# The short block's two output tiles: one tile's additions made first, and its rows sent in transfers of 64 on two queues

## The chip, the cores and the metric

One core of one Trainium2 chip runs the whole program. The metric is the device time of one execution in microseconds (us), taken as the median of several runs. The engines are PE (matrix products), DVE (vector), ACT (scalar), POOL (GpSimd) and SP (the sync engine, which here issues every DMA).

## The reference

Attention with a positional bias over 4 batches, 8 heads, 576 positions and head size 64, then two feed-forward layers over the 4 x 576 = 2304 tokens. Only the last one matters here:

```python
def _moe2_ref(x, w_in, w_out):           # x: (2304, 512), w_in: (512, 2048), w_out: (2048, 512)
    h = x @ w_in
    g = where(h >= 1, h, where(h <= -1, 0, (h + 1) ** 2 / 4))
    return g @ w_out                      # float32, (2304, 512)
```

## The kernel before, in words

The 576 positions are cut into five blocks (`BLK`, line 126): four of 128 positions, and the short one of 64 (`SJ`, number 4). The last layer takes the blocks in the order 0, 1, 2, 3, 4 (`ORDER`, line 808), the short one last. A block has its 128 positions of all four batches, so 512 tokens; the short one has 64 of each batch, so 256 tokens.

Block 0 is done by `h2_mm`, `g_mid`, `out_mm` and `out_store`. The others are done by halves (a "unit" below: 256 tokens; two units for each of blocks 1 to 3 and one for block 4, seven in all) with a seven-product scheme in the manner of Strassen. For each unit the loop at line 1146 runs over eight pairs of the hidden columns (`q`):

- `g_pair` (lines 1091 to 1113): PE makes the hidden values (`h2_half`, line 1085, 24 matmuls of 128x256 for a pair, into the three PSUM tiles `pm`); ACT and DVE apply the function (1102 to 1104); POOL makes four sums (1106 to 1109); ACT and DVE split the seven operands into two fp16 parts (1111, 1112).
- `out7` (line 1124): 21 matmuls of 128x256 add into the seven products m0 to m6. It runs two pairs behind `g_pair` (`gl=2`). The products lie in four PSUM banks, two tiles called `s`: m0 to m3 in one, m4 to m6 in the other. There are only these two tiles, so the next unit's first matmul into either must wait until the unit before has been read out of it.
- `store7` (lines 1126 to 1139), after the last pair of a unit: ACT copies m0, scaled, to SBUF (1133). DVE then makes seven additions (1136), each of 128x256, that form the two output tiles o1 and o2 of 128 rows x 512 columns. o2's right half, after the first addition, is a sum that others read, and it is overwritten by a later one. Then SP issues one transfer for each tile (1139).

In blocks 1 to 3 an output tile has 128 positions of one batch (`nr` = 128, `reps` = 1). In block 4 it holds 64 positions of two batches (`nr` = 64, `reps` = 2), so that transfer's pattern is 2 x 64 rows of 2 KB: the outer step goes from one batch to the next.

The instructions of each engine run in the order that a planner writes at build time; it goes by program order as priority and by its own forecast of when each instruction is ready. So DVE's additions for a unit can have other work between them.

Of the kernel before, what the change touches and what calls it, by code (L numbers as in the profile page):

```python
# [20 lines left out]
def kernel(ctx: ExitStack, tc: tile.TileContext, qt, kt, vr, small, mw1, mw2, mw3, mwo, win, wo2, out):  # L21
# [7 lines left out]
    V, A, G, T, SP = nc.vector, nc.scalar, nc.gpsimd, nc.tensor, nc.sync  # L29
    P = 128  # L30
    B, H, S, D = 4, 8, 576, 64
# [62 lines left out]
    def st(shape, dt, tag):  # L94
        return sb.tile(shape, dt, tag=tag, name=tag, bufs=BUFS.get(tag, 1))
# [69 lines left out]
    if True:  # L165
# [73 lines left out]
        for j in range(5):  # L239
            i0, n = BLK[j][0], BLK[j][1]  # L240
# [885 lines left out]
        def store7(y, sub, m, g):  # L1126
            i0, nr, n = BLK[ORDER[y]]
            k = c_ko[:, g:g + 1]
            o1, o2 = part[2 * (gcount[1] % 2)], part[2 * (gcount[1] % 2) + 1]
            gcount[1] += 1  # L1130
            lo, hi = slice(0, 256), slice(256, 512)
            m1 = st([P, S], F32, "sp")[:, :256]
            A.activation(m1, m[0], AF.Copy, scale=k)
            for dst, x, add in ((o2[:, hi], 1, m1), (o1[:, lo], 2, m1), (o2[:, lo], 3, o2[:, hi]), (o1[:, hi], 4, o2[:, hi]),
                                (o2[:, hi], 4, o2[:, lo]), (o1[:, hi], 5, o1[:, hi]), (o2[:, lo], 6, o2[:, lo])):
                V.scalar_tensor_tensor(dst, m[x], k, add, ALU.mult, ALU.add)
            reps = P // nr
            for c, o in ((2 * sub, o1), (2 * sub + 1, o2)):
                SP.dma_start(out.rearrange("(b i) d -> b i d", b=B)[c * reps:c * reps + reps, i0:i0 + nr], o)

        gcount.append(0)
        work = [(0, 0, ft) for ft in range(NF2)] + [(y, sub, q) for y in range(1, 5) for sub in range(BLK[ORDER[y]][2] // 256) for q in range(NP)]
# [3 lines left out]
        for x in range(len(work) + GL):  # L1146
# [19 lines left out]
            if x >= GL:  # L1166
                y, sub, ft = work[x - GL]
                if y == 0:
                    if ft % GROUP == 0:
                        accs[0] = acc4()  # L1170
                    end = ft % GROUP == GROUP - 1
                    out_mm(ORDER[0], ft, gls.pop(x - GL), accs[0], ft % GROUP == 0, end)
                    if end:
                        out_store(0, accs.pop(0), ft // GROUP, ft == GROUP - 1, ft == NF2 - 1)
                else:
                    if ft == 0:
                        accs[y] = [a[:, 256 * i:256 * i + 256] for a in acc4() for i in range(2)]
                    out7(ft, gls.pop(x - GL), accs[y], ft == 0, ft == NP - 1)
                    if ft == NP - 1:
                        store7(y, sub, accs.pop(y), NP - 1 + y)  # L1180
# [35 lines left out]
```

## Time and profile before

| | us |
|---|---|
| median of 3 runs | 1039.41 |
| lowest and highest of them | 1038.9, 1041.57 |
| the profiled execution | 1050.42 |
| its span, first to last instruction | 1048.6 |
| busy in the span: PE | 945.8 |
| DVE | 720.8 |
| ACT | 600.3 |
| POOL | 496.4 |

The profiled execution is 11.0 us longer than the median of the runs. Its span is 1.8 us shorter than its own time. Every time with a position in it ("at 1034.44") is counted from the first instruction of the span.

### The profile page before, as it was taken

How to read it: one execution, taken by the hardware profiler on the slowest of the kernel's cores; microseconds unless marked ns; L12 is line 12 of the kernel's file. 1: busy time of each engine (PE TensorE's matmuls, PEld its weight loads, DVE VectorE, ACT ScalarE, POOL GpSimd, SP SyncE). 2: the span in 40 equal slices, each digit the busy share in tenths (PEclk: the TensorE clock that was granted, in tenths of full speed). 3: DMA queues.
4: the chain of work that ended last, by engine and by line, in shares of the span. 5: the costliest groups of instructions: out<-in, count | busy, mean ns of one | idle time of the engine just before them, and what ended most of it. 6: DMA issues, size and time to landing. Idle time of an engine off the chain costs nothing. (4 is left out here: it accounts for less than half of the span.)

```text
span 1048.6 us, 25979 instructions
## 1 busy us (share of the span) xinstructions
PE 945.8 (90%) x10258; PEld 767.8 (73%) x10258; DVE 720.8 (69%) x1614; ACT 600.3 (57%) x1194; POOL 496.4 (47%) x721
## 2 busy tenths in 40 slices
PE   5779788798999999989899888989999999999993
PEld 5547667677888878777677777534588888888882
DVE  8977777776556677546455587898786677676662
ACT  4688864864565645768577687443344344344441
POOL 1022487665667764646457101976034344344340
PEclk7667889989999999999989999999999999999997
DMA  9795998998799978999989753010020010000000
GB/s 299 219 269 119 251 205 213 190 214 209 154 226 213 196 180 188 208 219 232 211 160 195 195 205 105 21 41 1 1 81 22 2 41 22 2 21 21 2 22 20
DMA packets 238910, 141.47 MB, mean 135 GB/s; under 512 B 187460, under 2 KB 217668, under 8 KB 238276
## 3 DMA queue, kind: packets, MB, share of 16 engines
q1 hardware_dynamic: 238788, 139.81, 57.3%
q8 instruction: 80, 1.31, 0.5%
q14 instruction: 42, 0.34, 0.1%
HBM read 79.68 MB, written 15.27 MB: 91 GB/s over the span
## 5 line engine op out<-in xcount | busy, mean ns | idle before, releaser
L775 PEld LDWEIGHTS <-aw 128*128 128x128 f16 x2160 | 193.2, 101 | 49.7 <-issue 28.2
L775 PE MATMUL pm<-xT,aw 128*128 128x256 f16 (+1 forms) x1944 | 219.6, 267 | 10.6 <-ACT hl L802 3.0
L698 POOL TENSOR_TENSOR phl<-sp,phl 128x512 f16<-128x512 f32 x136 | 161.5, 1188 | 0.0
L680 ACT ACTIVATE sp<-sp,mx 128x576 f32<-128x576 f32 x144 | 110.6, 768 | 79.9 <-DVE mx L678 79.5
L697 POOL TENSOR_TENSOR phl<-sp,phl 128x64 f16<-128x64 f32 x136 | 47.1, 346 | 208.8 <-ACT phl L696 132.8
L664 PE MATMUL s<-k,qz 64*128 64x288 f32 (+1 forms) x576 | 135.0, 458 | 10.3 <-DVE mx L678 8.2
L1102 ACT ACTIVATE sp<-pm,vec 128x256 f32<-128x256 f32 x112 | 61.3, 556 | 93.1 <-PE pm L1085 93.0
L678 DVE CUSTOM_DVE_ANT_0 sp<-s,ab 128x576 f32<-128x576 f32 x128 | 93.5, 752 | 30.5 <-POOL phl L698 12.6
L720 PEld LDWEIGHTS <-pt 128*128 128x128 f16 x1792 | 75.4, 102 | 35.2 <-DMA pt<-phl 22.7
L664 PEld LDWEIGHTS s<-k,qz 64*128 64x128 f32 (+1 forms) x576 | 72.7, 199 | 32.6 <-DVE mx L678 12.1
L696 ACT ACTIVATE phl<-sp 128x576 f16<-128x576 f32 x136 | 89.9, 673 | 3.3 <-DMA pt<-phl 2.5
L720 PE MATMUL pav<-v,pt 128*128 128x64 f16 x1568 | 72.8, 198 | 15.6 <-DMA pt<-phl 15.3
L797 PE MATMUL pm<-hh,wo 128*128 128x256 f16 x648 | 77.1, 273 | 6.7 <-ACT hl L802 3.1
L1085 PEld LDWEIGHTS <-ab 128*128 128x128 f16 x756 | 73.8, 98 | 9.4
L1106 POOL TENSOR_TENSOR hh<-hh 128x128 f32<-128x128 f32 x56 | 30.2, 540 | 106.3 <-DVE hh L1104 101.4
L1103 DVE SCALAR_TENSOR_TENSOR hh<-pm,vec,sp 128x256 f32<-128x256 f32 x112 | 52.7, 479 | 34.2 <-ACT sp L1102 34.0
L797 PEld LDWEIGHTS <-wo 128*128 128x128 f16 x648 | 61.6, 98 | 16.9 <-issue 9.3
L787 POOL TENSOR_TENSOR hh<-hm,hh 128x256 f16<-128x256 f32 (+1 forms) x60 | 43.0, 716 | 62.3 <-ACT hh L786 60.9
L782 DVE SCALAR_TENSOR_TENSOR hm<-pm,hm 128x256 f32<-128x256 f32 (+1 forms) x120 | 47.1, 393 | 33.9 <-PE pm L775 14.0
L1124 PEld LDWEIGHTS <-xT 128*128 128x128 f16 x588 | 57.5, 98 | 7.8 <-ACT xT L1111 1.2
L1124 PEld LDWEIGHTS <-wo 128*128 128x128 f16 x588 | 57.5, 98 | 6.7
L1107 POOL TENSOR_TENSOR hh<-hh 128x128 f32<-128x128 f32 x56 | 25.8, 460 | 72.6 <-DVE hh L1104 67.9
(281 smaller groups left out, 1990.4 us busy)
## 6 DMA issues: line engine op xcount, KB each, us to landing
k<-in_k_dram SPq DMA_DIRECT2D x64, 288.0 KB, 4.1
v<-v_d SPq DMA_DIRECT2D x24, 640.0 KB, 5.0
ws<-in_moe_w_out_dram SPq DMA_DIRECT2D x15, 512.0 KB, 5.0
ws<-in_moe_w_in_dram SPq DMA_DIRECT2D x9, 512.0 KB, 4.5
x_d<-hl SPq DMA_DIRECT2D x36, 128.0 KB, 3.0
qz<-in_q_dram SPq DMA_DIRECT2D x16, 256.0 KB, 5.3
ab<-in_moe_w_dram SPq DMA_DIRECT2D x8, 512.0 KB, 8.8
qz<-x_d SPq DMA_DIRECT2D x4, 1024.0 KB, 4.8
```

Of the source, the lines that this page charges most:

```text
L664: last_score[0] = T.matmul(sbox[i + r][:, c, :288], q[p, s if u.j == SJ else s // 2], k[p, 288 * c:288 * c + 288], start=True, stop=True)
L678: V.tensor_tensor_reduce(halves(sn), sbox.pop(i)[:, :, :288], halves(bias_sb[u.j][:, h]), -0.125, 3e38, ALU.add, ALU.min, mx)
L680: last_soft[0] = A.activation(pf, sn, AF.Exp, scale=-1.0, bias=mx, accum_out=u.sums[:, h:h + 1])
L696: A.activation(hl[:, :S], pf, AF.Copy)
L698: G.tensor_tensor(hl[:, S + 64:], pf[:, :512], hl[:, :512], ALU.subtract)
L720: T.matmul(u.pav[:, 64 * h:64 * h + 64], pt[:, c], v[:, sl, 64 * (h % 4):64 * (h % 4) + 64], **kw)
L775: T.matmul(o, wm[:, ft, i, wp, kk], x_rhs(key, xp, kk) if n == 256 else x_rhs(key, xp, kk)[:, c], start=(x == 0), stop=(x == 11))
L797: T.matmul(pm, wo16[:, ft, wp, P * d:P * d + P], hh[:, ft, hp], start=(ft == 0 and y == 0), stop=(ft == NF1 - 1 and y == 2))
L1085: T.matmul(pm, w[:, wp, kk], x2t[ORDER[y]][:, kk, xp, 256 * sub:256 * sub + 256], start=(x == 0), stop=(x == 11))
L1102: A.activation(r, pm, AF.Relu, scale=c_ch[:, f], bias=c_half)
L1103: V.scalar_tensor_tensor(t, pm, c_c[:, f], r, ALU.mult, ALU.max)
L1124: T.matmul(m[x], gl[:, gp, i], w[:, wp], start=(start and z == 0 and x % 2 == 0), stop=(stop and z == 2 and (x % 2 == 1 or x == 6)))
```

## The change

In `store7` the seven additions are put into another order, in all seven units: the ones that complete o1 come as numbers 2, 3 and 4, and the other three of o2 follow. The operands of each are the same. Each output tile is sent by one transfer for each batch in it: the first from SP, the second, if there is one, from ACT. Where `reps` is 1 (blocks 1 to 3) that is again one transfer of 128 rows from SP. In block 4 it is two transfers of 64 rows x 2 KB for each tile, one from SP and one from ACT, four instead of two.

```diff
-            for dst, x, add in ((o2[:, hi], 1, m1), (o1[:, lo], 2, m1), (o2[:, lo], 3, o2[:, hi]), (o1[:, hi], 4, o2[:, hi]),
-                                (o2[:, hi], 4, o2[:, lo]), (o1[:, hi], 5, o1[:, hi]), (o2[:, lo], 6, o2[:, lo])):
+            for dst, x, add in ((o2[:, hi], 1, m1), (o1[:, lo], 2, m1), (o1[:, hi], 4, o2[:, hi]), (o1[:, hi], 5, o1[:, hi]),
+                                (o2[:, lo], 3, o2[:, hi]), (o2[:, hi], 4, o2[:, lo]), (o2[:, lo], 6, o2[:, lo])):
                 V.scalar_tensor_tensor(dst, m[x], k, add, ALU.mult, ALU.add)
             reps = P // nr
             for c, o in ((2 * sub, o1), (2 * sub + 1, o2)):
-                SP.dma_start(out.rearrange("(b i) d -> b i d", b=B)[c * reps:c * reps + reps, i0:i0 + nr], o)
+                for r in range(reps):
+                    (A if r else SP).dma_start(out.rearrange("(b i) d -> b i d", b=B)[c * reps + r, i0:i0 + nr], o[nr * r:nr * r + nr])
```

Here `A` is ACT, `V` is DVE, `SP` the sync engine, `lo` and `hi` the left and right 256 columns; the second item of each entry is the number of the product.

## Rows read from the trace of the kernel before

**Rows 1.** Busy time by stage: us, PE, PEld, DVE, ACT, POOL, PEclk, DMA share, GB/s.

```profile
1000.00:1030.00 30.00, 29.12 (x268) 25.87 (x266) 17.95 (x31) 11.36 (x17) 12.47 (x24) 1.00 0.05 19
1030.00:1048.60 18.60, 1.56 (x15) 1.16 (x12) 3.15 (x8) 0.47 (x1) 0.00 (x0) 0.64 0.08 28
```

**Rows 2.** The chain that ended last, its end: start, us, what.

```profile
1031.33 0.48 ACT sp L1133
...
1031.84 1.67 DVE hm L1136 x4
...
1033.54 0.88 DVE hm L1136 x2
```

**Rows 3.** Timeline from 1034 on: start, us, engine, line, what.

```profile
1033.54 1.27 DVE L1136 SCALAR_TENSOR_TENSOR hm<-s,vec,hm 128x256 f32<-128x256 f32 x3
1034.44 1.30 SPq L1139 DMA_DIRECT2D out_dram<-hm  x2
```

**Rows 4.** What SP waited for after 1030: line, releaser, us, times, longest.

```profile
SPq L1212 <- DMA out_dram<-hm: 11.8, 1, 11.8
```

**Rows 5.** The DMA view from 1034 to 1049, 40 slices of 0.375 us.

```profile
DMA  0000010110111111111111111111111111100000
GB/s 0 0 0 0 22 22 22 33 33 22 22 44 44 55 49 49 55 49 49 55 49 49 55 49 49 55 55 44 55 55 49 49 55 49 49 11 0 0 0 0
DMA packets 260, 0.52 MB, mean 35 GB/s; under 512 B 4, under 2 KB 4, under 8 KB 260
```

**Rows 6.** The DMA view of a 128-row unit, 842.3 to 848, slices of 0.1425 us.

```profile
DMA  0000002799960000000499993000000000000000
GB/s 0 0 0 0 0 0 86 302 402 417 388 230 15 0 0 0 0 0 0 187 388 417 388 359 101 0 0 0 0 0 0 0 0 0 0 0 0 0 0 0
DMA packets 288, 0.52 MB, mean 92 GB/s; under 512 B 32, under 2 KB 32, under 8 KB 288
out_dram<-hh SPq DMA_DIRECT2D x2, 256.0 KB, 2.0
```

**Rows 7.** Line 1139: ns of an issue (min/median/max), first and last start; landing.

```profile
L1139 SPq DMA_DIRECT2D out_dram<-hm x8: 332/332/667, 803.1 to 1035.2; - x8
DMA to landing us min/median/max: 2.0/2.0/4.0
```

**Rows 8.** Line 310, 64-row loads at the program's start: ns of an issue; landing.

```profile
L310 SPq DMA_DIRECT2D ws<-in_v_dram x6: 487/1199/5053, 6.3 to 113.7; - x6
DMA to landing us min/median/max: 7.6/9.4/12.7
```

**Rows 9.** The program's first transfer and its first reader, in the timeline.

```profile
0.74 0.40 SPq L168 DMA_DIRECT2D sm<-in_small_dram  x1
2.57 0.23 DVE L205 TENSOR_SCALAR sc<-sm 128x8 f32<-128x8 f32 x1 [1.63 <-DMA sm<-in_small_dram]
```

**Rows 10.** Timeline of the first changeover between units, without POOL.

```profile
801.02 0.87 DVE L1136 SCALAR_TENSOR_TENSOR hm<-s,vec,hm 128x256 f32<-128x256 f32 x2
...
802.25 0.87 DVE L1136 SCALAR_TENSOR_TENSOR hm<-s,vec,hm 128x256 f32<-128x256 f32 x2
...
803.39 0.49 PE L1124 MATMUL s<-ab,wo 128*128 128x256 f16 x3
...
804.42 0.48 DVE L1136 SCALAR_TENSOR_TENSOR hm<-s,vec,hm 128x256 f32<-128x256 f32 x1
...
806.23 0.49 PE L1124 MATMUL s<-ab,wo 128*128 128x256 f16 x3
```

**Rows 11.** Line 1124: PE's waits (ns, first and last start) and its idle time.

```profile
L1124 PEldq EVENT_SEMAPHORE x6: 51/51/51, 801.5 to 998.3; - x6
its engine sat idle before it (us, times) until:
  ACT xT L1111: 2.0, 2
```

## The prediction

> **What bounds the kernel now.** I began with the busy time by stage, because a single bound for the whole span would mislead here. Up to 1030 PE is the bound: between 1000 and 1030 it is busy 29.12 of 30 us. In the last 18.6 us it works 1.56 us, DVE 3.15, ACT 0.47, and POOL nothing [rows 1]. So the program ends with some 14 us in which no engine computes, and whatever shortens that stretch shortens the program us for us.
>
> Next the end of the chain of waits and the timeline. ACT copies m0 at 1031.33; DVE's seven additions run from 1031.84 without other work among them [rows 2] and end at 1033.54 + 1.27 = 1034.81. SP issues the first tile's transfer at 1034.44 and is through with the second at 1034.44 + 1.30 = 1035.74 [rows 3]. From there SP waits 11.8 us, in one piece, for the output to land [rows 4], to about 1047.6; the closing steps take the remaining 1.0 us to 1048.6. That wait is the target.
>
> Is 11.8 us what 512 KB costs? The DMA view says no. In this stretch the DMA share is a steady 1 tenth, at about 52 GB/s, and 512 KB at 52 GB/s is 10.1 us [rows 5]. A unit of 128 positions sends the same 512 KB in two transfers of 256 KB at shares of 9 tenths and up to 417 GB/s, each within about 1 us, and each lands 2.0 us after its issue [rows 6]. 417 over 52 is 8, and two of sixteen engines is an eighth. The small packets say the same: 32 for two transfers there, which I read as one completion from each of 16 engines; 4 for two transfers here, two engines each [rows 5, 6]. The transfers differ in one thing: 128 rows against 2 x 64 rows. So the short block's data go through two DMA engines because the outer step of their pattern has two values, and both tiles queue on the same two.
>
> **The change part by part.** *The transfers.* Two transfers of 2 x 64 rows go; four of 64 rows come. I take a 64-row pattern to spread over the sixteen engines as a 128-row one does. Then o2's two halves are together the size of one 128-row transfer, 256 KB, and at 417 GB/s that is 0.6 us of traffic [rows 6]; issue to landing I take as 2.0 us, the median of the 128-row transfers of this line, whose extreme is 4.0 [rows 7]. One half alone has fewer bytes, but both share the engines. The only 64-row transfers in the trace are loads at the program's start, issue to landing 7.6 to 12.7 us [rows 8]; they stood behind megabytes of other loads, while at the end nothing else moves. So the bounds are 2.0 and 12.7, and I take the near one, since the nearest row in place, size and direction is that of the same output.
>
> The Trainium skill speaks against this part (DMA: Bandwidth & Descriptors, section "Rules for kernel authors"): of two transfers to disjoint partition halves it says "Don't bother — they serialize", one transfer of 128 partitions being better. Taken as it stands, that rule leaves the end at 1039.4; it supposes halves and whole on the same sixteen engines, and the trace shows the whole on two. The same page (section "Why a DMA increments its semaphore by 16 and not by 1") lets the outermost step choose the engines: 2 gives two, and 64 would give sixteen. The 2 and the 128 agree with the completions counted above; no row shows a 64-row transfer in the clear.
>
> *The second queue.* ACT has issued no transfer before. Its issue cost is not in the trace; SP's lie between 0.33 and 0.67 us for this line [rows 7], and being shorter could not bring the end forward by more than 0.33. I take SP's 0.33. A first use of a queue is bounded by SP's own: issued at 0.74, used at 2.57, so 1.83 us in all [rows 9], no more than a warm one. ACT has nothing after the copy of m0 [rows 2], so nothing is queued behind its waits; SP has nothing behind these transfers but the final wait.
>
> *The order of the additions.* An addition that waits for nothing new begins 0.40 us after the one before: three in 1.27 us with 0.48 for the last, (1.27 - 0.48) / 2 [rows 3, 10]. The fourth began at 1031.84 + 3 x 0.40 = 1033.04, the fifth at 1033.54 [rows 2]: 0.50, because it overwrites what the fourth reads. So an addition that depends on its direct predecessor costs 0.10 more. Before there is one such; after there are three (o1's right half twice, o2's left half into its right half, and that read before the left half is overwritten). The last addition ends at 1034.81 + 0.20 = 1035.01. o1 is complete after the fourth instead of the sixth addition, at about 1033.6 instead of 1034.4; but o2 comes last, so this brings nothing to the end beyond keeping both queues free. If the planner puts another addition between, the 0.20 is not paid.
>
> *The sum.* o2's transfers are issued at 1035.04 (0.03 after the last addition, as now) and land at 1037.04, against 1047.6. That is 10.5 us less; the closing steps stay at 1.0. Profiled execution: 1050.42 - 10.5 = 1039.9. It stands 11.0 us above the median of the runs; its extra time I take to lie outside this stretch, since the rate of two engines doesn't depend on being watched: 1039.41 - 10.5 = 1028.9.
>
> *The six other units.* Their transfers keep pattern and queue. The new order also works where PE is the bound. The next unit's products need the PSUM tiles. In the first changeover the third addition, the last reader of m0 to m3, begins at 801.02 and ends 0.48 later, at 801.5, which is where PE's wait stands [rows 10, 11], and PE uses that tile at 803.39: 1.9 us of slack. After the change m3 is read by the fifth addition. That now starts at 802.25, ending at 802.7, still 0.7 us early; the cover is PE's work on the next pairs' hidden values. The last addition ends at 804.90 and its tile is used at 806.23, a slack of 1.3 us against a delay of at most 0.2 [rows 10]. PE's idle time before line 1124 is 2.0 us in all, and none of it is put down to the additions [rows 11]. I take nothing for these units.
>
> **The rivals.**
>
> *Changeovers cost a little.* The planner already leaves the last addition until 804.42, 1.3 us after the sixth ended [rows 10]. If it does that to o2's three additions, m3 is read at about 804.9 at the latest, 1.5 us after PE wants the tile. If PE's other work fills half of that, six changeovers cost 6 x 0.75 = 4.5 us: 1033.4. For it: three additions in place of one can be pushed behind other work. Against: their program order is still ahead of the next unit's.
>
> *Slower.* The same mechanism in full, at its place, the release of m0 to m3. Each changeover would have to cost over (10.5 + 3.1) / 6 = 2.3 us, so the fifth addition would have to end after 803.39 + 2.3 = 805.7, 4.2 us later than the third does now [rows 10]. At 2.6 us each: 1039.41 - 10.5 + 15.6 = 1044.5. Against it: PE has 14 matmuls of other work between the two parts and took the tiles with slack.
>
> *No gain.* The 64-row halves stay narrow, or queue one behind the other as slowly as the busy loads, up to 12.7 us from issue to landing [rows 8]: landing at 1035.04 + 12.7 = 1047.7, and 1039.5. That is also the case in which the edit doesn't do what it says. For it: the only 64-row rows are slow. Against: the DMA share there and here.
>
> **How the numbers follow.** Forecast 0.85; small changeover cost 0.07; no gain 0.04; slower 0.04. A measurement of this kernel tells some 0.3%, 3.1 us, from no change. So faster 0.92, same 0.04, slower 0.04. The range: up, a landing at the line's extreme of 4.0 us (2.0), ACT's issue at 0.67 (0.3) and the spread of the runs (about 0.8) make 1032.0. Down, the 0.2 not paid, a landing at 1.83 (0.2), PE's wait before the last products closing by a new order of work (1.0: the 2.0 us are two parts of one wait, of load and of product [rows 11]) and 0.7 of spread make 1026.8. It leaves the three rivals out, 0.15.
>
> **What would show it.** In the changed kernel: after 1034 a DMA share of several tenths for about a microsecond and 64 small packets for the short block instead of 4; SP's last wait near 1.5 us, not 11.8; the first tile's issue 0.8 us before the last addition's end or more; landing of line 1139 near 2.0 on both queues; and PE still without idle time put down to the additions. A last wait of 10 us or more would make the transfers' part wrong; idle PE between 800 and 1006 would make the changeovers' part wrong.

## The result

| us | before | after |
|---|---|---|
| median of the runs | 1040.95 (8 runs, 1038.9 to 1043.11) | 1031.84 (8 runs, 1027.67 to 1036.81) |
| the profiled execution | 1050.42 | 1027.98 |
| its span | 1048.6 | 1026.2 |

The ratio of the times is 0.9907, with a 95% interval of 0.9886 to 0.9928: between 7.5 and 11.9 us faster, 9.1 by the medians. The forecast was 10.5 us, to 1028.9.

The two profiled spans differ by 22.4 us, more than twice that. Where the rest lies is seen from the start of ACT's copy of m0 in each unit. Here is the profile's line for that copy (1133), of before and then of after; the last two times are its first and last start:

```profile
L1133 ACT ACTIVATE sp<-s,vec x7: 462/474/475, 799.6 to 1031.3; 128x256 f32<-128x256 f32 x7
```

```profile
L1133 ACT ACTIVATE sp<-s,vec x7: 462/474/475, 787.3 to 1018.6; 128x256 f32<-128x256 f32 x7
```

The first copy is the first instruction of a unit's output. Up to there the lists of instructions are the same, and after is 12.3 us earlier: that is not the change. Three further profiles of kernels with the same instructions up to there (two of the changed kernel, one of an experiment below) start it at 789.0, 790.7 and 799.9, so the stretch varies by that much between executions. TensorE's mean granted clock up to 786 is 0.93 in the profile of before and 0.95 in that of after. From the first copy to the last it is 231.7 against 231.3 us. From the last copy to the end it is 17.3 against 7.6. So the change shows as 9.7 us at the end and 0.4 us before the last copy.

The end of after, in the timeline (start, us, engine, line, what), then SP's waits, then the DMA view from 1018.5 to 1026.5 in 40 slices of 0.2 us. They answer to [rows 2 to 6].

```profile
1018.60 0.47 ACT L1133 ACTIVATE sp<-s,vec 128x256 f32<-128x256 f32 x1 [2.29 <-PE s L1124]
1019.11 0.88 DVE L1136 SCALAR_TENSOR_TENSOR hm<-s,vec,sp 128x256 f32<-128x256 f32 x2 [1.61 <-ACT sp L1133]
1019.90 2.17 DVE L1136 SCALAR_TENSOR_TENSOR hm<-s,vec,hm 128x256 f32<-128x256 f32 x5
1021.18 1.41 SPq L1140 DMA_DIRECT2D out_dram<-hm  x2
1021.19 1.47 ACTq L1140 DMA_DIRECT2D out_dram<-hm  x2
```

```profile
SPq L1213 <- DMA out_dram<-hm: 2.3, 1, 2.3
```

```profile
DMA  0000000000000000000499997877930000000000
DMA packets 320, 0.52 MB, mean 66 GB/s; under 512 B 64, under 2 KB 64, under 8 KB 320
q1 hardware_dynamic: 160, 0.26, 13.2%
q10 hardware_dynamic: 160, 0.26, 8.8%
out_dram<-hm SPq DMA_DIRECT2D x2, 128.0 KB, 2.6
out_dram<-hm ACTq DMA_DIRECT2D x2, 128.0 KB, 2.9
```

The reader is to see four things. SP waits 2.3 us for the output instead of 11.8. The DMA share is 7 to 9 tenths for 2 us instead of 1 tenth for 11. There are 64 small packets, sixteen for each of four transfers, instead of 4. And the seven additions end at 1019.90 + 2.17 = 1022.07, 3.5 us after the copy of m0 started, just as before; from there to the end of the span it is 4.1 us, against 13.8. This last stretch is called the tail below. It repeats within 0.15 us from profile to profile (4.1, 4.0 and 4.0 in three of the changed kernel), while the stretch before the first unit varies by 12 us; so the tail is what tells the experiments apart. The ratios of the times stand beside it.

### The profile page after: what moved, and what is told of

It reads as the page before. It is cut to its first block, busy times and chain, and to the rows that moved or that the text cites. A ratio compares the mean times of both kernels' runs of the same rounds, so it can differ in the third digit from the quotient of the medians.

```text
span 1026.2 us, 25997 instructions
## 1 busy us (share of the span) xinstructions
PE 933.7 (91%) x10258; PEld 759.3 (74%) x10258; DVE 719.3 (70%) x1614; ACT 600.6 (59%) x1194; POOL 498.3 (49%) x721
## 5 line engine op out<-in xcount | busy, mean ns | idle before, releaser
L775 PE MATMUL pm<-xT,aw 128*128 128x256 f16 (+1 forms) x1944 | 215.9, 264 | 7.4 <-ACT hm L780 2.8
L664 PE MATMUL s<-k,qz 64*128 64x288 f32 (+1 forms) x576 | 131.4, 452 | 12.1 <-DVE mx L678 9.9
L720 PEld LDWEIGHTS <-pt 128*128 128x128 f16 x1792 | 72.2, 100 | 34.3 <-DMA pt<-phl 22.9
L1106 POOL TENSOR_TENSOR hh<-hh 128x128 f32<-128x128 f32 x56 | 33.3, 595 | 106.6 <-DVE hh L1104 88.6
L1107 POOL TENSOR_TENSOR hh<-hh 128x128 f32<-128x128 f32 x56 | 26.4, 471 | 69.0 <-DVE hh L1104 62.0
```

The costliest lines, as they stand in the source:

```text
L664: last_score[0] = T.matmul(sbox[i + r][:, c, :288], q[p, s if u.j == SJ else s // 2], k[p, 288 * c:288 * c + 288], start=True, stop=True)
L720: T.matmul(u.pav[:, 64 * h:64 * h + 64], pt[:, c], v[:, sl, 64 * (h % 4):64 * (h % 4) + 64], **kw)
L775: T.matmul(o, wm[:, ft, i, wp, kk], x_rhs(key, xp, kk) if n == 256 else x_rhs(key, xp, kk)[:, c], start=(x == 0), stop=(x == 11))
```

## The experiments

The theory under test: the whole gain comes from the number of DMA engines, which the outer step of the pattern sets. The rivals: the second queue carries it; the new order, which lets o1 leave earlier, carries it; any pattern of two levels is slow, whatever its outer count.

In the table "2 of 2 x 64" means two transfers of 2 x 64 rows each. `two_queues` and `rows62` were executed once each, so for them the tail alone is read.

| kernel | additions | the short block's transfers | tail, us | ratio to before, 95% interval |
|---|---|---|---|---|
| before | old | 2 of 2 x 64 rows, SP | 13.8 | |
| order_only | new | 2 of 2 x 64, SP | 13.3 | 0.9982 (0.9954 to 1.0011) |
| two_queues | new | 2 of 2 x 64, SP and ACT | 13.1 | |
| rows62 | new | 4 of 62 and 4 of 2 rows, SP | 13.2 | |
| rows64_sp | old | 4 of 64, SP | 5.0 | 0.9925 (0.9900 to 0.9950) |
| rows64_sp_order | new | 4 of 64, SP | 4.4 | 0.9896 (0.9872 to 0.9920) |
| the change (after_again, after_third) | new | 4 of 64, SP and ACT | 4.0 | 0.9910 (0.9885 to 0.9934), 0.9908 (0.9881 to 0.9934) |
| interleaved | new | 2 of 64 x 2, SP | 3.5 | 1.0051 (1.0027 to 1.0075) |
| interleaved_act | new | 2 of 64 x 2, SP | 3.5 | 0.9899 (0.9875 to 0.9924) |

**The parts of the change, one by one.** `order_only` keeps the transfers of before (the edit is against the changed kernel; in all these diffs `out...` stands for the rearranged output):

```diff
-                for r in range(reps):
-                    (A if r else SP).dma_start(out...[c * reps + r, i0:i0 + nr], o[nr * r:nr * r + nr])
+                SP.dma_start(out...[c * reps:c * reps + reps, i0:i0 + nr], o)
```

> Edit: the new order of the additions alone; the short block still leaves in two transfers of 2 x 64 rows from SP. By the tail is meant the time from the end of DVE's last addition to the end of the span: 13.84 us before, 4.13 us after. Theory (engine count: the whole gain comes from the 64-row patterns running on sixteen engines instead of two): the tail stays near 13.8 us, since both tiles still queue on two engines; starting the first transfer 0.4 us sooner than before may take up to 0.5 off. Time ratio to before 0.998 to 1.002. Rival O (the first tile leaving earlier carries the gain): tail near 6 to 8 us, ratio 0.991 to 0.994.

The time cannot be told from that of before. SP's last wait hardly moves:

```profile
1019.89 2.17 DVE L1136 SCALAR_TENSOR_TENSOR hm<-s,vec,hm 128x256 f32<-128x256 f32 x5
SPq L1212 <- DMA out_dram<-hm: 11.6, 1, 11.6
```

The tail is 0.5 us shorter (span 1035.36). o1's transfer left 0.9 us ahead of the last addition's end instead of 0.4, so the two engines had that much more done. In the tail the order alone carries a twentieth of the gain.

`rows64_sp` keeps the old order and sends four transfers of 64 rows, all from SP (the edit is against the kernel before):

```diff
-                SP.dma_start(out...[c * reps:c * reps + reps, i0:i0 + nr], o)
+                for r in range(reps):
+                    SP.dma_start(out...[c * reps + r, i0:i0 + nr], o[nr * r:nr * r + nr])
```

> Edit: the 64-row transfers alone, all four from SP, with the old order of the additions. Theory (engine count): tail 4.2 to 5.0 us, a little over the 4.13 of the full change because four issues of about 0.5 us stand one behind the other on SP; ratio 0.990 to 0.993. Rival Q (the second queue carries the gain, because one queue feeds its transfers one after the other): tail above 8 us, ratio 0.995 or more. The issue time tells a side question: 0.33 us per issue if the longer issues of 0.50 to 0.57 us of the full change come from two engines issuing together, about 0.55 if they belong to the 64-row pattern.

Timeline and DMA view of its end:

```profile
1021.71 2.17 DVE L1136 SCALAR_TENSOR_TENSOR hm<-s,vec,hm 128x256 f32<-128x256 f32 x5
1023.52 2.48 SPq L1140 DMA_DIRECT2D out_dram<-hm  x4
```

```profile
DMA packets 320, 0.52 MB, mean 60 GB/s; under 512 B 64, under 2 KB 64, under 8 KB 320
out_dram<-hm SPq DMA_DIRECT2D x4, 128.0 KB, 2.3
```

With one queue and the old order the tail is 1028.85 - 1023.88 = 5.0 us (1028.85 is the span). So 8.9 of the 9.7 us come with the pattern alone. Four issues take 2.48 us on SP, about 0.6 each: the longer issue goes with these transfers and not with two engines issuing together.

`rows64_sp_order` is the changed kernel with SP in place of ACT, and `after_again` is the changed kernel itself. The edit of the first, against the changed kernel:

```diff
-                    (A if r else SP).dma_start(...)
+                    SP.dma_start(...)
```

> Edit: the full change without ACT: new order, four 64-row transfers from SP. Theory (engine count): tail 3.9 to 4.8 us, so within 0.7 us of the full change, and the same time within 0.1%; the second queue saves SP's issue time and costs some waiting of the two queues on the same engines. Rival Q: tail above 8 us.

> The changed kernel unaltered, on the same chip as the three others. Both theories: ratio to before 0.989 to 0.993, tail 4.1 us. In the first profile the stretch before the first changed instruction was 12.3 us shorter than in the profile of before although the instructions are the same. If that is variation between executions, another profile puts this stretch anywhere between 787 and 800 us, and the profile of before on the same chip can be as short; if the change reaches it in a way the lists of instructions do not show, it stays near 787.

The last additions of `rows64_sp_order`, whose span is 1039.16 us:

```profile
1032.56 2.17 DVE L1136 SCALAR_TENSOR_TENSOR hm<-s,vec,hm 128x256 f32<-128x256 f32 x5
```

The tail without ACT is 4.4 us and with it 4.0 and 4.1: the order brings 4.97 - 4.44 = 0.5 us on top of the pattern, the second queue 0.3 to 0.4 more. Both are under what the times can tell; the intervals of the three 64-row kernels overlap. The second profile of the changed kernel has its first copy of m0 at 789.0, and `rows64_sp_order`, with the same instructions up to there, at 799.9; `rows64_sp`, which has the old order of before, has it at 788.7. So the 12.3 us of the first comparison are variation.

**Is it the number of engines, and what sets it?** `two_queues` sends one 2 x 64 transfer from each queue (this edit and the next ones are against the changed kernel):

```diff
-                for r in range(reps):
-                    (A if r else SP).dma_start(out...[c * reps + r, i0:i0 + nr], o[nr * r:nr * r + nr])
+                (A if nr < P and c % 2 else SP).dma_start(out...[c * reps:c * reps + reps, i0:i0 + nr], o)
```

> Edit: against the changed kernel, one transfer of 2 x 64 rows for each tile again, o1 from SP and o2 from ACT. Theory (engine count, and a 2 x 64 pattern takes the same two engines from either queue): tail near 13 us, as with one queue (13.29 with this order of additions), since 512 KB still pass two engines at 52 GB/s in all. If ACT's queue takes two other engines, the tails overlap: o2 alone, 256 KB at 52 GB/s, 5.0 us of traffic, so a tail near 8 us. Rival Q (the second queue carries the gain): 8 us or less.

The DMA view from 1025.8 to 1043, slices of 0.43 us:

```profile
DMA  0000000002011101111111111111111111100000
GB/s 0 0 0 0 0 0 0 0 0 38 19 29 29 38 29 52 52 48 52 52 52 52 48 52 52 48 52 52 48 57 48 52 52 48 52 14 0 0 0 0
q1 hardware_dynamic: 130, 0.26, 4.7%
q10 hardware_dynamic: 130, 0.26, 3.9%
```

Two queues, and still 52 GB/s and 1 tenth in all, which is what two engines moved before [rows 5]. With two other engines for ACT's queue a tail near 8 us was expected. So both transfers go through the same two engines. The tail is 13.1 us against 13.3 with one queue: the second queue by itself is worth 0.1 us here.

`rows62` sends plain transfers of one level, but of 62 and 2 rows:

```diff
-                    (A if r else SP).dma_start(out...[c * reps + r, i0:i0 + nr], o[nr * r:nr * r + nr])
+                    for x in ((slice(0, 62), slice(62, 64)) if nr < P else (slice(0, nr),)):
+                        SP.dma_start(out...[c * reps + r, i0 + x.start:i0 + x.stop], o[nr * r + x.start:nr * r + x.stop])
```

> Edit: against the changed kernel, each 64 rows go from SP in two plain transfers, of 62 and of 2 rows. Theory (the number of engines is a divisor, of at most 16, of the row count, as the Trainium skill has it in DMA: Bandwidth & Descriptors: 62 = 2 x 31 gives two): tail of 11 us or more, nearly all of the old wait, although no pattern has two levels: 256 rows of 2 KB over two engines at 80 ns each are 10 us. Rival (a plain one-level transfer spreads over sixteen engines whatever its row count): tail 5 to 7 us, the four more issues of about 0.5 us on SP.

The last additions and the DMA view from 1023.7 to 1041 (the span is 1040.42):

```profile
1025.04 2.17 DVE L1136 SCALAR_TENSOR_TENSOR hm<-s,vec,hm 128x256 f32<-128x256 f32 x5
DMA  0000000011010111111111111111111111000000
DMA packets 272, 0.52 MB, mean 30 GB/s; under 512 B 16, under 2 KB 16, under 8 KB 272
```

With 62 rows instead of 64 the old rate is back: a share of 1 tenth, and 16 small packets for eight transfers, two each. So the rival that a plain transfer spreads over sixteen engines whatever its row count falls. The Trainium skill (DMA: Bandwidth & Descriptors, section "Why a DMA increments its semaphore by 16 and not by 1") gives the number of engines as the largest number up to 16 that divides the outermost counts of both sides, here the rows of the output and the partitions of the tile; these runs agree for outer counts of 2, 62, 64 and 128.

`interleaved` tests the other side: a pattern of two levels with 64 outside. The short block's tokens are put in the order (pair of batches, position, batch), so that a tile goes out as 64 x 2 rows. To get that order PE writes the first layer's products of the short block with a step of two elements in PSUM, and ACT reads and writes with that step in line 802.

```diff
-            o = pm if key[0] != SJ else pm.rearrange("p (b t) -> p b t", b=B)
+            o = pm if key[0] != SJ else pm.rearrange("p (y t z) -> p y z t", y=2, z=2)
...
-                for r in range(reps):
-                    (A if r else SP).dma_start(out...[c * reps + r, i0:i0 + nr], o[nr * r:nr * r + nr])
+                dst = out...[c * reps:c * reps + reps, i0:i0 + nr]
+                SP.dma_start(dst.rearrange("b i d -> i b d") if reps > 1 else dst, o)
```

> Edit: against the changed kernel, the short block's tokens stand in the order (pair of batches, position, batch) instead of (batch, position), from the first feed-forward layer on, so that a tile of 128 rows goes out in one transfer from SP again, its pattern on the output side 64 x 2 rows instead of 2 x 64: the same rows of 2 KB, the same two-level pattern, only its outer step has 64 values. ACT's scaling of the short block in line 802 reads and writes every second element. Theory (the outer step's count sets the number of engines): 64 x 2 runs on sixteen engines, 32 small packets for the two transfers, an issue near 0.33 us, landing 2.0 to 2.1 us, and a tail of 3.1 to 3.4 us, 0.7 to 1.0 below the changed kernel; the time within 0.2% of it. Rival (any two-level pattern is slow): tail near 13.3 us.

The tail was 3.5 us, the shortest so far: the same rows, again in a pattern of two levels, but with the 64 outside. The DMA view from 1040 to 1051:

```profile
DMA  0000000000000000000000000000896897000000
DMA packets 288, 0.52 MB, mean 48 GB/s; under 512 B 32, under 2 KB 32, under 8 KB 288
out_dram<-hm SPq DMA_DIRECT2D x2, 256.0 KB, 2.4
```

There are 32 small packets for two transfers: sixteen engines each. Nor does the number of transfers set the tail: eight are slow in `rows62`, and two are fast here. The sizes were missed: landing 2.4 us instead of 2.0, an issue of 0.56 to 0.64 us instead of 0.33, and the time, which I had within 0.2% of the changed kernel, is 0.5% above before. Line 775 tells why, this kernel first and then after; the columns are ns (min/median/max), first and last start:

```profile
L775 PE MATMUL pm<-masks,aw x216: 376/421/421, 579.5 to 629.8; 128*128 128x256 f16 x108
```

```profile
L775 PE MATMUL pm<-masks,aw x216: 269/273/421, 568.9 to 602.9; 128*128 128x256 f16 x108
```

These 216 matmuls take 421 instead of 273 ns each. They overlap one another, so what they cost is read from the stretch that they fill: from the first start to the last it is 50.3 us instead of 34.0, 16.3 us more. PE is busy for 50.2 of the 50.7 us up to the end of the last one, against 29.6 of 34.3 in after, so here PE has become the bound. In the times this kernel is some 15 us slower than the changed one (ratios to before of 1.0051 and 0.991, at 1043.69 us for before).

`interleaved_act` gets the same order of tokens from the writes of line 802 alone:

```diff
-                A.activation(t[:, c], pm[:, c], AF.Copy, scale=c_rb[:, b:b + 1])
+                d_ = t.rearrange("p (y t z) -> p y t z", y=2, z=2)[:, b // 2, :, b % 2] if key[0] == SJ else t[:, c]
+                A.activation(d_, pm[:, c], AF.Copy, scale=c_rb[:, b:b + 1])
```

> Edit: against the changed kernel, the short block's order of tokens (pair of batches, position, batch) again, for one transfer of 64 x 2 rows per tile from SP, but the products of the first feed-forward layer keep their order in PSUM: only ACT's write in line 802 puts every second element. The run before it, in which PE wrote the products with that step, had a tail of 3.50 us and was slower over all, with 216 products of the short block at 421 instead of 273 ns. Theory (the strided writes of PE were what made that run slower, the 64 x 2 transfers are good): line 775 back at 273 ns, line 802's 16 writes for the short block at most 0.05 us longer each, tail 3.5 us, 0.5 to 0.6 below the changed kernel, ratio to before 0.989 to 0.992. Rival (the other order of tokens costs elsewhere): ratio above 0.995.

> The changed kernel unaltered, on the same chip and in the same minutes as the run above: tail 4.0 to 4.1 us, ratio to before 0.989 to 0.993; the difference between the two, about 0.5 us, is under what the times can tell, so the tail in the profile decides.

Its lines 775, 803 (802 of before) and its end:

```profile
L775 PE MATMUL pm<-masks,aw x216: 269/273/421, 573.2 to 607.0; 128*128 128x256 f16 x108
```

```profile
L803 ACT ACTIVATE hl<-pm,vec x80: 307/360/417, 240.6 to 659.1; 128x128 f32<-128x128 f32 x64, 128x64 f32<-128x64 f32 x16
```

```profile
1024.00 2.17 DVE L1137 SCALAR_TENSOR_TENSOR hm<-s,vec,hm 128x256 f32<-128x256 f32 x5
1025.28 1.48 SPq L1141 DMA_DIRECT2D out_dram<-hm  x2
```

PE is back at 273 ns. The 16 writes of the short block (128x64) are those with the step; they take 307 to 417 ns, and 308 to 417 in the profile of before, so the step costs ACT nothing that shows. The tail is 1029.66 - 1026.17 = 3.5 us (1029.66 is the span), and the ratio of 0.9899 shows that the gain is back. On the same chip the medians are 1031.37 for this kernel and 1031.17 for the changed one: the 0.5 us by which its tail is shorter cannot be told in the times. It needs no second queue.

## Why the prediction was right, and where its sizes were off

**What bounds the end: right.** The end of the program was a wait for two DMA engines, and traffic at an eighth of the rate was rightly read from the share, the rate and the small packets [rows 5, 6]. `rows64_sp` and `two_queues` separate that reading from the queue, `order_only` from the order, `rows62` from the plain pattern and `interleaved_act` from the number of levels.

**The sum.** Forecast were 10.5 us. Measured are 9.7 from the last copy to the end and 0.4 before it, so 10.1 by the profiles, and 9.1 by the times (7.5 to 11.9). That the total came so near is in part luck: the landing was taken 1.0 us too short, while 0.2 us for the additions was not paid and 0.4 us was gained before the last copy, where nothing was forecast (10.5 - 1.0 + 0.2 + 0.4 = 10.1). The time itself, 1031.84, is 2.9 us above the forecast of 1028.9 and only just below the upper bound of 1032.0; 1.5 of the 2.9 lie in the base, whose median was 1039.41 over three runs and is 1040.95 over eight. The terms, one by one:

- *The transfers* were sized too small. I took 2.0 us from issue to landing, from the 128-row transfers [rows 7]. The last landing in the changed kernel came 3.0 us after its issue. Line 1140 of after (ns of an issue; landing min/median/max):

```profile
L1140 SPq DMA_DIRECT2D out_dram<-hm x8: 332/332/548, 790.0 to 1022.1; - x8
L1140 ACTq DMA_DIRECT2D out_dram<-hm x2: 561/567/573, 1021.2 to 1022.1; - x2
DMA to landing us min/median/max: 2.0/2.1/3.0
```

  A 64-row transfer from SP lands in 2.3 us when SP alone issues (`rows64_sp`), 0.3 more than a 128-row one though it is half the size; its issue takes about 0.25 us longer. In the changed kernel both queues feed the same sixteen engines at once, and the landing rises to 2.6 (SP) and 2.9 us (ACT) in the median. Together that is the missing 1.0 us. SP's last wait is 2.3 us, where 1.5 was the sign to look for. All these landings lie within the bounds I kept, 2.0 to 12.7.
- *The order of the additions* was to cost 0.20 us and cost nothing: the last five additions take 2.17 us before and after. o1's transfers are issued at 1021.18, which is when the fifth addition ends (1019.90 + 2 x 0.39 + 0.48 = 1021.16), not the fourth; so the planner had put one of o2's additions between o1's two. This is the case I named and did not take.
- *"This brings nothing to the end beyond keeping both queues free"* was too little: the order is worth 0.5 us in the tail by each pair of kernels that differ in it alone (13.8 to 13.3, 5.0 to 4.4). In both pairs SP alone issues, and o1's transfers start 0.5 us sooner, ahead of o2's. With both queues and 64 rows no such pair was run.
- *ACT's issue* at SP's 0.33 us: it is 0.57, within the bounds of 0.33 and 0.67. SP's own rose as well, to 0.50 and 0.55.
- *The other six units* at nothing: right. From the first copy of m0 to the last it is 231.7 us in both profiles of the old order (before, `rows64_sp`) and 231.3 in all nine of the new, and the 0.4 us lie after the sixth copy, in the short block's own unit (34.8 against 34.4). PE's idle time before line 1124 is now 1.2 us instead of 2.0, and as before it is put down to ACT alone [rows 11]:

```profile
its engine sat idle before it (us, times) until:
  ACT xT L1111: 1.2, 2
```

  That is the wait before the last products, counted twice, for the weight load and for the product; it shrank by 0.4 us, which is the whole difference. The prediction named this closing for its lower bound (1.0 us) and not in the sum. Why the new order shortens that wait was not traced. The release of m0 to m3 never held PE up, so both rivals built on it fall.

**The rule against.** That two transfers of partition halves aren't worth making, since both spread over all sixteen engines (the Trainium skill, DMA: Bandwidth & Descriptors, section "Rules for kernel authors"), does not hold where the whole runs on two engines: the split alone is worth 8.9 us. Where a whole transfer uses all sixteen, as in `interleaved_act`, one transfer is indeed better than the halves: its tail is 0.5 us shorter than that of the changed kernel, and 0.9 shorter than that of `rows64_sp_order`, which sends the halves from SP alone.

**The base.** I laid the 11.0 us by which the first profile exceeded the median outside the end of the program. That stands: the stretch before the first unit varies by 12 us between profiles, while the tail repeats (13.8 us here, and 13.1 to 13.3 in the three other kernels on two engines, whose executions were 6 to 13 us shorter).

## What to carry to other kernels

Look at how the program ends: a last wait of many microseconds at a DMA share of 1 tenth, with few small packets per transfer, says that a transfer runs on few engines, and the cure is the count in its outer step, not another queue. Give the outer step a count that spreads, as 64 and 128 did here and 2 and 62 did not, by cutting the transfer or by choosing the order of the rows so that the long dimension is outside. And judge a change at the end of a program by the stretch from the last computation to the end, which repeats within 0.15 us here, where whole executions of one kernel vary by about ten.

## What the runs showed of the hardware that I had not expected

- Transfers of 62 rows run on two engines and those of 64 on sixteen; from the same queue and with the same order the tails are 13.2 and 4.4 us.
- An SP issue of a 128-row transfer took 0.33 us in the middle of the program, while those of 64 rows and of 64 x 2 rows at the end took 0.5 to 0.65. The place alone does not make them long: in `rows62` the first transfer of 62 rows was issued at the same place in 0.32 us. What it is in the pattern stays open.
- ACT's queue uses the same two engines as SP's for a 2 x 64 pattern: 52 GB/s in all with both queues at work.
- PE's products written with a step of two elements in PSUM take 421 instead of 273 ns for 128x256, and a run of nine takes 2.11 instead of 1.15 us (the first nine of line 775's 216 in `interleaved` and in after), while ACT's writes to SBUF with that step show no extra time.
